# A recurrent attention layer beside a dense layer: weights kept in PSUM as 32-bit words, their copies shared between two engines, queries turned earlier, one load for two row blocks, a wider kept part

## The chip, the cores and the metric

The kernel runs on one core of a Trainium2 chip. The metric is the device time of the whole kernel in microseconds. A core has TensorE (PE; PEld is its loading of weights), VectorE (DVE), ScalarE (ACT), GpSimd (POOL) and SyncE (SP), which here does nothing but start DMA transfers. Transfers are also started from ACT's and POOL's queues.

## What is computed

Two branches over the same normalised input are added to the input. B is a dense layer with GELU; A is attention over segments of 32 tokens, in which each segment also reads 8 memory tokens, and the first 8 rows of its output are the memory of the next segment. So A is a chain of 64 segments, one after the other.

```
xn = layernorm(x)                                   # 2048 x 1024, bf16
out = x + A(xn) + gelu(xn @ w1 + b1) @ w2 + b2      # w1: 1024 x 3584
A:  mem = mem0                                      # 8 x 1024
    for s in range(64):
        h = concat(mem, xn[32 s : 32 s + 32])       # 40 rows
        q, k, v = h @ Wq, h @ Wk, h @ Wv            # 32 heads of 128
        p = softmax(mask(q k^T / sqrt(128)))
        o = (p v) @ Wo                              # back to 1024 columns
        mem = o[0:8];  out of segment s = o[8:40]
```

## The kernel before, in words

**Two stages.** The first stage normalises x, turns it (tokens along the free dimension) and does the dense layer in four groups of 512 tokens. It leaves the turned rows of every segment in a DRAM tensor `hr_d` (columns 0 to 255 of a segment's slot) and the dense result plus input, the residual, in columns 256 to 511 of the slot after it. Then the recurrence runs over 64 segments. To spare PE work, a main tile of 32 rows holds the 8 memory rows and 24 tokens of a segment, and the 8 tokens left over are worked off for four segments together ("left", names with an L, 32 rows per group of four, `i4 = s % 4`): their K, Q, V products are spread over the four segments, and once per group (`left_o`, at `i4 == 1`) the output product is twice as wide.

**Weights.** The four projections are 64 units of 512 KB ([128, 2048] bf16). A segment uses them in the order of `pass_order`: half passes K0, Q0, K1, Q1, V0, V1 of 8 units each, then 16 units of the output product O. SBUF doesn't hold all of them. 46 stay resident; 18 are streamed (`PLACED`, letter S). Six slots form a ring: when PE is done with a streamed unit, `unit_done` calls `start_stream` for the slot that is free now, and SP starts the load of a later unit into it. Two of the 18 never come from DRAM after segment 0: `IN_PSUM` (Q, 4, 0) and `IN_BANKS` (the sixth streamed unit of O, its 15th) are held in four PSUM banks (`kept`) and are copied into their slot by VectorE (L247, two copies of 128x1024 bf16 each); they are started three places later than a load would be, at O's 8th unit for IN_BANKS and K0's first for IN_PSUM. Of a third, `PART` (the fifth streamed of O), the first 512 columns stay in SBUF (`part_home`), and only the rest is loaded (L249). `keep` puts the weights into PSUM in segment 0: PE turns each 128x128 block, ACT and DVE copy the turned blocks to SBUF, PE turns them back into the bank.

**Order.** The program is written out by hand (a manual schedule): each engine runs its instructions in the order of the program, and a half pass takes a table `at`, which says after which unit what else is put in. In segment 0, SP's queue holds, in this order: the last resident units (`xt2`, `xt3`, whose slots are first written out to DRAM as `R_n`), the load of `d_oL` (the second half of IN_BANKS, L605), then the streams. After Q0 the program puts `keep(IN_BANKS)`, the load of `part_home` (L925), and the turning of Q.

**A segment.** A half pass ends with a cast from PSUM by ACT (L758) and, for K and Q, a transposition in 32x32 blocks by VectorE (L772, L939). The queries of the 8 left tokens are put beside the main ones by `q_left` (L794), after Q's half pass. `keep_q` (L801) saves queries that later segments need from being overwritten. `scores` (L808: PE, then Exp on ACT, then two minima on DVE), `sums` (L836: PE sums, Ln and two Exp on ACT, then two products on DVE, L862 and L866, which divide the probabilities) and `values` (L873) run inside later half passes: scores of half 0 after the first unit of Q1, its sums after the last; scores of half 1 after V1's first unit. After V1, the next segment's turned rows are loaded (`load_x_rows`, L259) and, after the first unit of O, the residual (`load_res`, L969): two loads of 64 KB from the same 128 rows of `hr_d`, on ACT's queue up to segment 4, on POOL's from there. O's result is cast (L1002), and `put_mem` (L282 on PE, L286 on DVE) writes the new memory rows into the turned rows, with which the next segment begins. The residual is added (L1017) and POOL stores the rows. For `i4 == 2` they go to a scratch tensor `outM_d` (L1049) and from there to the output (L1052), both on POOL.

**SBUF at fixed places.** Below the pools lie POOL's descriptor space (`SCRATCH`, 512 bytes per partition) and 3584 bytes of small tiles: `half_home` (its columns hold `part_home`, the residual `res_home` and the probabilities `pr_all`), `hr_home` (the turned rows), `pd_main`, `pd_left`, `small_consts`.

Of the kernel before, what the change touches and what calls it, by code (L numbers as in the profile page):

```python
# [11 lines left out]
U32 = mybir.dt.uint32  # L12
# [36 lines left out]
SCRATCH = 512  # L49
SMALL = 3584  # L50
# [4 lines left out]
PART_COLS = 512  # L55
# [31 lines left out]
def kernel(  # L87
# [51 lines left out]
    hr_home = nc.alloc_sbuf_tensor_at("hr_home", [P, 256], BF16, offset=SCRATCH + 2048)  # L139
    pd_main = nc.alloc_sbuf_tensor_at("pd_main", [P, 320], BF16, offset=SCRATCH + 2560)  # L140
    pd_left = nc.alloc_sbuf_tensor_at("pd_left", [P, 128], BF16, offset=SCRATCH + 3200)
    small_consts = nc.alloc_sbuf_tensor_at("small_consts", [P, 16], BF16, offset=SCRATCH + 3456)

    part_home, res_home, pr_all = half_home[:, 0:PART_COLS], half_home[:, 512:768], half_home[:, 768:1024]

    bd, off = small_consts[:, 0:4], small_consts[:, 4:8].bitcast(F32)

# [3 lines left out]
    ctx.enter_context(tc.manual_schedule())  # L151

# [8 lines left out]
    ident = pd_main[:, 0:P]  # L161
# [77 lines left out]

    def start_stream(slot):  # L240
# [4 lines left out]
        if unit in kept_in:  # L245
            for c0, bank in kept_in[unit]:
                nc.vector.tensor_copy(out=t[:, c0:c0 + 1024], in_=bank)  # L247
        elif unit == PART:
            nc.sync.dma_start(out=t[:, PART_COLS:], in_=copies[unit])  # L249
        elif unit in copies:  # L250
            nc.sync.dma_start(out=t[:, :], in_=copies[unit])
        else:
            fetch(t[:, :], unit)
# [4 lines left out]
    def load_x_rows(s, eng=nc.sync):  # L258
        eng.dma_start(out=hr_home[:, :], in_=hr_d[s, :, 0:256])  # L259
        nxt["hT"] = hr_home.rearrange("p (k t) -> p k t", k=KT)  # L260
# [32 lines left out]
    with tc.tile_pool(name="ma", bufs=2) as ma, tc.tile_pool(name="mps", bufs=6, space=PSUM) as mps:  # L293
# [191 lines left out]
        for tg in range(4):  # L485
# [81 lines left out]
            else:  # L567
# [7 lines left out]
                put_mem(o_sb, nxt["hT"], mps.tile([P, 512], F32, name="ps"))  # L575
                pss = [mps.tile([P, 512], F32, name="ps") for _ in range(6)]
# [28 lines left out]
                nc.sync.dma_start(out=d_oL[:, :], in_=Wo_v[:, h + 1, :])  # L605
# [6 lines left out]
    with tc.tile_pool(name="late", bufs=1) as late, \  # L612
# [28 lines left out]
        kept = banks.tile([P, 4, 1024], BF16, name="kept")  # L641

        def copy_bits(out, in_):

            nc.vector.tensor_single_scalar(out=out, in_=in_, scalar=0, op=ALU.bitwise_or)

        def keep(unit, c0, w, bank):

            turned = [late.tile([P, 512], BF16, name=f"VL{n}").rearrange("p (k t) -> p k t", k=4) for n in range(2)]
            for n in range(2):  # L650
                for k in range(4):
                    nc.tensor.transpose(trs[n][:, k, :], w[:, 512 * n + P * k:512 * n + P * (k + 1)], ident)
                (nc.scalar.copy if n else nc.vector.tensor_copy)(out=turned[n], in_=trs[n])
            for n in range(2):
                for k in range(4):
                    c1 = 512 * n + P * k
                    nc.tensor.transpose(kept[:, bank, c1:c1 + P], turned[n][:, k, :], ident)
# [32 lines left out]
        for s in range(NSEG):  # L690
# [145 lines left out]
            def sums(u):  # L836
# [17 lines left out]
                for b in (1, 0):  # L854
# [3 lines left out]
                    )  # L858
                pdA = pd_main.rearrange("p (c b q) -> p c b q", c=4, b=2)
# [38 lines left out]
            def o_product(unit, t, acc):  # L898
# [4 lines left out]
                for k in range(2):  # L903
                    for jq in range(DM // n):
                        r, c0 = n // 8 * jq, DM * k + n * jq
                        w_t = part_home if unit == PART and c0 < PART_COLS else t
                        nc.tensor.matmul(  # L907
                            acc[r:r + n // 8, 0:n],
                            lhsT=lhs[:, 4 * (i % 4) + 2 * u + k, :],
                            rhs=w_t[:, c0:c0 + n],  # L910
                            start=(unit == O_UNITS[0] and k == 0),
                            stop=(unit == O_UNITS[-1] and k == 1),
                            tile_position=(0, r),
                        )


# [4 lines left out]
            psQ, psQL = half_pass("Q", 0, left_q[0], {})  # L921
            if first:
                keep(IN_BANKS, 1024, d_oL, 2)
                keep(IN_BANKS, 0, half_home, 3)
                nc.sync.dma_start(out=part_home, in_=Wo_v[:, 4 * PART[1] + 2 * PART[2], 0:PART_COLS])  # L925
                copy_bits(mixed[:, 468:512].bitcast(U32), mask.bitcast(U32))
                for t in outs:
                    nc.vector.memset(t[:, :, 0:32], 0.0)
                turn_qL(psQL, 0)
            q_left(0)  # L930
            turn_q(psQ)
            if left_q[0] and not first:
                keep_q(0)
# [10 lines left out]
            elif left_k[0]:  # L944
                at[1] = [lambda: turn_kL(psKL, 0)]
            psQ1, psQ1L = half_pass("Q", 1, left_q[1], at)
            if first:
                turn_qL(psQ1L, 1)
            q_left(1)
            turn_q(psQ1)  # L950
            if left_q[1] and not first:
                keep_q(1)
# [7 lines left out]
            at = {0: [lambda: scores(1)], 4: [lambda: sums(1)]}  # L960
# [4 lines left out]

            def load_res():
                st["res"] = res_home
                eng = nc.scalar if s < 5 else nc.gpsimd
                eng.dma_start(out=st["res"][:, :], in_=hr_d[s + 1, :, 256:512])  # L969
# [5 lines left out]
            if not final:  # L975
                load_x_rows(s + 1, nc.scalar if s < 5 else nc.gpsimd)
            if first:
# [9 lines left out]
            at.setdefault(0, []).append(load_res)  # L987
# [105 lines left out]
```

## Time and profile before

The three timed runs gave 1892.51, 1891.93 and 1899.58 us (median 1892.51). The profiled execution took 1888.7 us, with a span of 1887.0 from the first to the last instruction, at a granted TensorE clock of 0.994.

| engine | busy us | share | instructions |
|---|---|---|---|
| PE | 1729.5 | 92% | 32255 |
| PEld | 940.0 | 50% | 32275 |
| DVE | 921.3 | 49% | 2222 |
| ACT | 637.6 | 34% | 1356 |
| POOL | 277.2 | 15% | 538 |

| queue | packets | MB | share of 16 engines |
|---|---|---|---|
| q1 (from SP) | 199292 | 593.57 | 83.0% |
| q0 (from POOL) | 16320 | 17.52 | 2.8% |
| q10 (from ACT) | 4096 | 2.64 | 0.5% |
| instructions (q8, q14) | 317 | 4.66 | 1.0% |

| transfers | count | KB each |
|---|---|---|
| streamed units of K, V, O, Q | 320, 256, 256, 128 | 512 |
| PART | 64 | 384 |
| turned rows, residual (POOL) | 58, 59 | 64 |

Shares are of the span of the slowest core, here the only one. A busy PE isn't PE at its peak, because matmuls overlap and their ends are modelled. A wait for several semaphores is put down to the one that came last. Numbers with an L are lines of the kernel.

### The profile page before, as it was taken

What the parts mean: (1) busy time and instruction counts of PE and PEld (TensorE: products, weight loads), DVE (VectorE), ACT (ScalarE), POOL (GpSimd) and SP (SyncE); (2) the same over time, 40 slices, a digit from 0 to 9 for tenths busy, and PEclk for the clock granted to TensorE, in tenths of its full rate; (3) what the DMA queues carried; (4) which work ended last, traced back from release to release, by engine and by line L of the source; (5) the groups of instructions that cost most, each with busy time, mean ns of one, the idle gap of its engine ahead of it and who ended that gap; (6) DMA issues with size and microseconds to landing.
All of it is one profiled execution on the core that took longest, in us unless ns stands there. A gap on an engine that the chain in (4) does not pass through costs nothing.

```text
span 1887.0 us, 72995 instructions
## 1 busy us (share of the span) xinstructions
PE 1729.5 (92%) x32255; PEld 940.0 (50%) x32275; DVE 921.3 (49%) x2222; ACT 637.6 (34%) x1356; POOL 277.2 (15%) x538
## 2 busy tenths in 40 slices
PE   7999999997998989999999999899999999988987
PEld 3444444444454545455555555455545454555544
DVE  6657474603454444444454445444444454444443
ACT  6334352502333333333333333333333333333332
POOL 0000000000341111111121111212121111111112
PEclk9999999998999999999999999999999999999999
DMA  9821211498999999999999999999999999999998
GB/s 337 269 52 45 55 47 50 172 351 278 401 395 377 372 377 356 378 391 395 391 392 383 387 369 390 370 386 387 385 398 386 392 398 380 387 380 369 376 379 325
DMA packets 220025, 618.39 MB, mean 328 GB/s; under 512 B 47243, under 2 KB 65595, under 8 KB 219708
## 3 DMA queue, kind: packets, MB, share of 16 engines
q1 hardware_dynamic: 199292, 593.57, 83.0%
q0 software_dynamic: 16320, 17.52, 2.8%
q8 instruction: 252, 4.13, 0.9%
q10 hardware_dynamic: 4096, 2.64, 0.5%
q14 instruction: 65, 0.53, 0.1%
HBM read 599.39 MB, written 30.34 MB: 334 GB/s over the span
## 4 chain that ended last, share of the span: by engine, by line
PE 67%; DMA 19%; DVE 7%; ACT 3%; issue 3%; POOL 0%; ACTq 0%; DVEq 0%; POOLq 0%; SPq 0%
PE acc L714 32%; PE ps L503 10%; PE acc L907 10%; DMA u<-Wc_K 9%; PE ps L552 8%; DMA u<-Wc_O 5%; DMA u<-Wc_Q 3%; PE ps L587 2%; ACT mixed L855 2%; PE acc L881 2%; DVE b_oL L772 1%; DMA outL_d<-half_home 1%; DVE pd_main L862 1%; PE mixed L816 1%; DVE u L247 1%
## 5 line engine op out<-in xcount | busy, mean ns | idle before, releaser
L714 PE MATMUL acc<-u,hr_home 128*32 128x512 bf16 x11520 | 781.5, 382 | 32.4 <-DMA u<-Wc_K 13.6
L714 PEld LDWEIGHTS <-hr_home 128*32 128x32 bf16 x12288 | 350.8, 97 | 321.5 <-issue 72.1
L714 PE MATMUL acc<-u,hrL 128*32 128x512 bf16 x2880 | 256.3, 381 | 12.4 <-issue 6.1
L503 PE MATMUL ps<-u 128*128 128x512 bf16 x896 | 194.9, 380 | 2.6 <-ACT u L387 2.6
L907 PE MATMUL acc<-u,d_oL 128*32 128x256 bf16 (+1 forms) x3552 | 177.2, 292 | 12.3 <-DMA u<-Wc_O 7.9
L247 DVE COPY u<-kept 128x1024 bf16<-128x1024 bf16 x254 | 163.3, 685 | 25.7 <-PE acc L907 9.1
L552 PE MATMUL ps<-u 128*128 128x512 bf16 x657 | 146.2, 379 | 0.8
L907 PEld LDWEIGHTS <-b_oL 128*32 128x32 bf16 (+1 forms) x3552 | 109.1, 98 | 75.0 <-issue 40.9
L503 PEld LDWEIGHTS <-u 128*128 128x128 bf16 x896 | 87.9, 98 | 108.4 <-issue 3.1
L907 PEld LDWEIGHTS <-d_oL 128*32 128x32 bf16 (+1 forms) x3552 | 104.4, 99 | 63.8 <-issue 20.7
L862 DVE TENSOR_TENSOR pd_main<-half_home,mixed 128x320 bf16<-128x320 bf16 x128 | 62.5, 488 | 150.1 <-ACT mixed L855 147.6
L907 PE MATMUL acc<-u,b_oL 128*32 128x256 bf16 (+1 forms) x1665 | 108.7, 290 | 19.3 <-DVE u L247 8.8
L714 PEld LDWEIGHTS <-hrL 128*32 128x32 bf16 x3072 | 90.4, 96 | 66.3 <-issue 24.7
L772 DVE STREAM_TRANSPOSE b_oL<-b_oL 128x512 bf16<-128x512 bf16 x128 | 90.6, 708 | 66.8 <-ACT b_oL L758 66.8
L907 PE MATMUL acc<-W_O,b_oL 128*32 128x256 bf16 (+1 forms) x1776 | 108.3, 289 | 4.9 <-issue 4.6
L758 ACT CAST kT<-acc 128x512 bf16<-128x512 f32 x64 | 37.5, 586 | 219.7 <-PE acc L714 219.7
L259 POOL DMA_DIRECT2D hr_home<-hr_d x58 | 32.7, 564 | 528.7 <-PE acc L714 528.7
L552 PEld LDWEIGHTS <-u 128*128 128x128 bf16 x672 | 65.3, 98 | 77.4 <-DVE g_u L519 0.4
L758 ACT CAST b_oL<-acc 128x512 bf16<-128x512 f32 x128 | 75.2, 588 | 80.5 <-PE acc L714 80.5
L833 DVE TENSOR_TENSOR half_home<-half_home,mixed 128x96 bf16<-128x96 bf16 (+1 forms) x256 | 37.6, 188 | 127.4 <-ACT half_home L828 127.3
L1002 ACT CAST d_oL<-acc 128x256 bf16<-128x256 f32 (+1 forms) x63 | 26.9, 427 | 214.2 <-PE acc L907 214.2
L855 ACT ACTIVATE mixed<-mixed,small_consts 128x160 f32<-128x160 f32 x256 | 94.3, 368 | 8.4
(129 smaller groups left out, 2033.3 us busy)
## 6 DMA issues: line engine op xcount, KB each, us to landing
u<-Wc_K SPq DMA_DIRECT2D x320, 512.0 KB
u<-Wc_V SPq DMA_DIRECT2D x256, 512.0 KB
u<-Wc_O SPq DMA_DIRECT2D x256, 512.0 KB
u<-Wc_Q SPq DMA_DIRECT2D x128, 512.0 KB
u<-Wc_O SPq DMA_DIRECT2D x64, 384.0 KB
u<-in_B_w_dram SPq DMA_DIRECT2D x14, 512.0 KB
u<-in_A_Wq_dram SPq DMA_DIRECT2D x14, 512.0 KB
u<-in_A_Wv_dram SPq DMA_DIRECT2D x12, 512.0 KB
```

The source lines that it names most:

```text
L247: nc.vector.tensor_copy(out=t[:, c0:c0 + 1024], in_=bank)
L503: nc.tensor.matmul(ps[:, :].rearrange("p (s t) -> p s t", t=SEG), lhsT=w1_sb[fb // 14 * 8 + kt][:, (fb % 14) * P:(fb % 14 + 1) * P], rhs=x ...
L552: nc.tensor.matmul(ps[:, :], lhsT=gts[fc // 4][:, fc % 4, t * P:(t + 1) * P], rhs=w2_sb[fc // 2][:, fc % 2, cs], start=(fc == 0), stop=(fc ...
L587: nc.tensor.matmul(pss[2 * t + nb][:, :], lhsT=gts[fc // 4][:, fc % 4, t * P:(t + 1) * P], rhs=w2_sb[fc // 2][:, fc % 2, nb * 512:nb * 512 ...
L714: nc.tensor.matmul(o, lhsT=lhs[:, i, :], rhs=m, start=(i == seq[0]), stop=(i == seq[-1]), tile_position=(0, 32 * j),)
L758: cp(out=out, in_=ps.rearrange("p (h e) -> p h e", e=32))
L772: nc.vector.transpose(out=home, in_=home)
L833: nc.vector.tensor_tensor(out=p, in0=p, in1=m[:, None, :].to_broadcast([P, 4, n]), op=ALU.min)
L855: nc.scalar.activation(out=mixed[:, 160 * b:160 * b + 160], in_=mixed[:, 0:160], func=ACT.Exp, scale=-1.0, bias=off[:, b:b + 1],)
L862: nc.vector.tensor_tensor(out=pdA.rearrange("p c b q -> p b c q"), in0=prA[:, None, :, :].to_broadcast([P, 2, 4, 40]), in1=dd, op=ALU.mult,)
L881: nc.tensor.matmul(oV[r][:, c, :, :], lhsT=V[q, c * P:(c + 1) * P], rhs=pdA[q, c, :, :], start=(c == 0), stop=False, skip_group_check=True ...
L907: nc.tensor.matmul(acc[r:r + n // 8, 0:n], lhsT=lhs[:, 4 * (i % 4) + 2 * u + k, :], rhs=w_t[:, c0:c0 + n], start=(unit == O_UNITS[0] and k ...
```

## The change

1. `PART_COLS` goes from 512 to 768: of PART's 2048 columns 768 stay in SBUF and 1280 are loaded per segment. The product of L907 takes the tile in which the border falls in two parts of 256 columns.
2. `keep` copies the weights to PSUM bit for bit, as 512 words of 32 bits, in one VectorE instruction per bank. IN_BANKS is kept before the first half pass of segment 0 instead of after Q0; the load of `d_oL` goes to where `put_mem` is done in the first stage, ahead of the last resident units in SP's queue.
3. Of the two copies of a kept unit into its slot, VectorE does the first as words and ScalarE the second as bf16.
4. `q_left` and `keep_q` go into the half pass of Q (after its third and fourth unit), ahead of the turning of Q; the two divisions of half 0 (`normalize`) go after the turning of Q1.
5. `load_x_rows` loads 512 columns, rows and residual together (segment 0's own rows excepted), after V1; `load_res` goes. `res_home` lies in `hr_home` now.
6. The transfer from `outM_d` to the output goes from POOL's to SP's queue and to the next segment, after the third unit of O.
7. `SCRATCH` goes from 512 to 384 bytes; `pd_left` and `small_consts` move into a pool.

```diff
-SCRATCH = 512
-SMALL = 3584
+SCRATCH = 384
+SMALL = 3712
...
-PART_COLS = 512
+PART_COLS = 768
...
             for c0, bank in kept_in[unit]:
-                nc.vector.tensor_copy(out=t[:, c0:c0 + 1024], in_=bank)
+                if c0:
+                    nc.scalar.copy(out=t[:, c0:c0 + 1024], in_=bank.bitcast(BF16))
+                else:
+                    copy_bits(t[:, c0:c0 + 1024].bitcast(U32), bank.bitcast(U32))
...
     def load_x_rows(s, eng=nc.sync):
-        eng.dma_start(out=hr_home[:, :], in_=hr_d[s, :, 0:256])
+        n = 512 if s else 256
+        eng.dma_start(out=hr_home[:, 0:n], in_=hr_d[s, :, 0:n])
...
                 put_mem(o_sb, nxt["hT"], mps.tile([P, 512], F32, name="ps"))
+                nc.sync.dma_start(out=d_oL[:, :], in_=Wo_v[:, h + 1, :])
...
         def keep(unit, c0, w, bank):
 
-            turned = [late.tile([P, 512], BF16, name=f"VL{n}").rearrange("p (k t) -> p k t", k=4) for n in range(2)]
-            for n in range(2):
-                for k in range(4):
-                    nc.tensor.transpose(trs[n][:, k, :], w[:, 512 * n + P * k:512 * n + P * (k + 1)], ident)
-                (nc.scalar.copy if n else nc.vector.tensor_copy)(out=turned[n], in_=trs[n])
-            for n in range(2):
-                for k in range(4):
-                    c1 = 512 * n + P * k
-                    nc.tensor.transpose(kept[:, bank, c1:c1 + P], turned[n][:, k, :], ident)
+            copy_bits(kept[:, bank, :].bitcast(U32), w.bitcast(U32))
...
+            if first:
+                keep(IN_BANKS, 1024, d_oL, 2)
+                keep(IN_BANKS, 0, half_home[:, :], 3)
+                nc.sync.dma_start(out=part_home, in_=Wo_v[:, 4 * PART[1] + 2 * PART[2], 0:PART_COLS])
...
             psK, psKL = half_pass("K", 0, left_k[0], {})
...
-            psQ, psQL = half_pass("Q", 0, left_q[0], {})
+            at = {} if first else {2: [lambda: q_left(0)]}
+            if left_q[0] and not first:
+                at[3] = [lambda: keep_q(0)]
+            psQ, psQL = half_pass("Q", 0, left_q[0], at)
...
-            q_left(1)
+                q_left(1)
             turn_q(psQ1)
+            normalize(0)
...
-            at = {0: [lambda: scores(1)], 4: [lambda: sums(1)]}
+            at = {0: [lambda: scores(1)], 4: [lambda: sums(1), lambda: normalize(1)]}
...
-            at.setdefault(0, []).append(load_res)
+            if i4 == 3:
+                at.setdefault(2, []).append(rows_of_main)
...
-                small.append(lambda o=o, r=r: nc.gpsimd.dma_start(out=o, in_=r))
+                rows_of_main = lambda o=o, r=r: nc.sync.dma_start(out=o, in_=r)
```

## The prediction

> **What bounds the kernel now.** I read the profile in this order: the DMA rows of the 40 slices, the stage windows, the records of single DMA packets, the chain of waits at the start of the recurrence, the waits. Page, part 2:
>
> ```profile
> DMA  9821211498999999999999999999999999999998
> GB/s 337 269 52 45 55 47 50 172 351 278 401 395 377 372 377 356 378 391 395 391 392 383 387 369 390 370 386 387 385 398 386 392 398 380 387 380 369 376 379 325
> ```
>
> From slice 11 on (some 470 us to the end) the 16 DMA engines are never below 90%. The dense half ahead of it is TensorE's, with DMA at a tenth or two; the change hardly touches it. Windows (length; busy us of PE, PEld, DVE, ACT, POOL; clock; DMA share; GB/s):
>
> ```profile
> 445.00:450.00 5.00, 3.06 (x64) 1.62 (x56) 3.16 (x8) 1.69 (x5) 0.00 (x0) 1.00 0.71 234
> 450.00:455.00 5.00, 4.60 (x56) 2.02 (x60) 1.87 (x4) 0.00 (x0) 0.00 (x0) 0.66 0.23 61
> 455.00:460.00 5.00, 4.74 (x124) 2.38 (x116) 1.49 (x4) 1.89 (x5) 0.00 (x0) 1.00 0.56 188
> 460.00:465.00 5.00, 4.82 (x144) 3.71 (x140) 2.97 (x6) 1.46 (x4) 0.71 (x1) 1.00 0.84 242
> ...
> 900.00:1000.00 100.00, 93.36 (x2176) 53.21 (x2172) 49.40 (x119) 33.96 (x79) 16.80 (x32) 1.00 1.01 393
> ```
>
> Steady segments have a DMA share of 1.01, so DMA sets their period. The casts of L1002, one at each segment's end, start from 465.6 to 1858.9 us: 62 periods of 22.47 us. VectorE is half busy and ScalarE a third. PE shows 93%, but its matmuls overlap (382 ns each, four started every 0.21 us), so this isn't PE at its limit: it waits often, and briefly. Counting in the packet records how many of 16 packets are in service at each ns between 500 and 1800 us leaves 2.0% of engine time free, 26 us: all that anything but DMA could still win there. The exception is segment 0 (418.9 to 465.6 us), where the windows above show idle DMA. Its chain:
>
> ```profile
> 419.54 8.30 DMA R_n<-u
> ...
> 428.34 4.43 DMA d_oL<-in_A_Wo_dram
> ...
> 432.82 0.41 PE mixed L652 x4
> ...
> 438.51 0.56 DVE qL L758
> ...
> 439.11 4.31 PE acc L714 x30
> ```
>
> SyncE's queue stands until 427.9 us for the write of R_n, then loads d_oL; PE waits for d_oL only to transpose it into PSUM, and the second half pass of K starts 20 us after the first.
>
> **What the Trainium skill says.** "ScalarE: Activation LUTs", What ACT_TABLE_LOAD costs: an ACTIVATE with immediate scale and bias is 186 ns + 0.833 ns per element. The trace agrees: casts from PSUM take 372 ns at 256 columns, 586 at 512. "VectorE: DVE Perf Modes", Why PSUM operands drop a tier: 32-bit data in PSUM goes at single rate. The trace's word copies into PSUM (L645) agree: 200 ns at 64 words, 267 at 128, so 1.05 ns a word. "DMA: Bandwidth & Descriptors", Issuing engines are not separate DMA queues: SP, ACT and POOL share the same 16 DMA engines; the one share near 1.00 agrees. The same page, Why a DMA increments its semaphore by 16 and not by 1: a DMA runs on the largest k up to 16 that divides the slowest dimension of both sides; from SP always on the lowest-numbered k, from POOL on k that rotate. The trace fits k = 4 for outM to out, whose slowest dimension is 4: it went as 12 packets of 4096 bytes, not a multiple of 16. Which engines they were, it doesn't show.
>
> **The change part by part.**
>
> *768 columns kept.* The load of PART shrinks from 384 to 320 KB: 128 packets of 2560 instead of 3072 bytes, once per segment. Mean packet times between 500 and 1800 us: 2048 bytes 86.4 ns, 3072 128.1, 4096 168.3. Halfway, 2560 takes 107.3. Saving: 128 x 20.8 ns / 16 engines = 0.166 us; with the medians (84, 121) 0.148; by bytes, 65.5 KB at 385 GB/s, 0.170. I take 0.16 us, times 64 loads = **-10.2 us**. It lies on the path, DMA being the bound. The wider product of L907 is cut in two for one tile in 16 segments: the same columns stream, nothing.
>
> *Weights kept as words.* Gone from segment 0: 64 transposes and 8 copies, with PE's waits between them (425.2 to 429.4, and from 432.8 until PE gets its bank at 439.1 after the qL cast queued behind). In their place four VectorE copies of 512 words, 267 + 384 x 1.05 = 0.67 us each: two ahead of segment 0, where VectorE is idle for 4.2 us before L772 at 423.1, two beside the Q pass. PE then runs into the SyncE queue: the first load after 427.9 us lands some 6 us later (estimate: 1.2 MB with what is ahead of it, 3.1 us at 400 GB/s, plus 2.9, which d_oL took beyond the 0.78 MB then queued: 432.8 - 427.9 - 2.0); PE would be there at 431, so segment 0 becomes DMA-bound from 428 on. What is saved is the DMA idle time after that: (0.29 + 0.77 + 0.44 + 0.16) x 5 = 8.3 us in the windows above. I take 8.0, and 0.5 for the 256 KB of d_oL, which move to before 420 us where DMA stood at 0.6, less 64 KB more for part_home: **-8.5 us**. Bounds: -4 (a second wait, such as the hrL load of 5.6 us) to -10.
>
> *Copies back shared.* Per segment four copies of 685 ns on VectorE (L247, two pairs) become two of 0.67 there and two on ScalarE. No row shows a ScalarE copy of 1024 columns: 586 + 512 x 0.833 = 1.01 us. A pair is ready after 1.01 instead of 1.37 us. Behind it on ScalarE stand the kT cast and L1002, before which ScalarE is idle 219.7/64 and 214.2/63 = 3.4 us: hidden. PE's wait for these copies is 8.8 us in all, part of the 2% slack: **0**, bounds -3 to +1.
>
> *Queries first.* q_left (0.15 to 0.20 us) and keep_q (0.20 to 0.27) move into the pass, beside its matmuls. The divisions (0.49 + 0.28) of half 0 now queue on VectorE behind the transposition of L772, which itself waits for ScalarE's 0.59 us cast. Before: Ln and two Exp, 1.1 us, divisions and q_left 0.8, transposition 0.63. Now 1.1, cast 0.59, transposition 0.63: PE's scores come 0.2 us earlier, values(0) 0.1 later, and where a qL cast follows (one segment in four) the bank comes free 0.4 later. All inside PE's slack: **0**, bounds -6 (part of the 16.3 us of the wait below) to +6 (16 x 0.4).
>
> *One load for rows and residual.* On ACT in the first five segments, on POOL afterwards. The bytes stay and a 64 KB load is already 16 packets of 4096, so DMA gains nothing; POOL saves an issue of 0.55 us, hidden. But put_mem (L286) now waits for 128 KB, one more packet per engine and one of the stream between: 0.33 us later. Landing is 5.2 us now. Behind the waiting L286 stand L1017 and the next copies on VectorE, and PE's next pass waits for it. Segment by segment, PE's last put_mem matmul ends between 0.6 us before and 3.4 after the landing; 0.3 us more adds 2.3 us over all segments. Half is hidden by DMA: **+1**, bounds 0 to +6 (0.9 us later, as if both came one after the other: 12.6, halved).
>
> *Rows of main on SP.* The store outM to out (one segment in four) leaves POOL, whose 5.3 us wait for outM goes; on SP it is issued 16 us later and waits for nothing; the issue, about 0.6 us like SP's other DRAM copies, falls into SyncE's waits for slots. It is 96 packets of 512 bytes (27 ns from the ACT queue). Spread evenly: 0.0. On the same four engines: 24 x 27 = 0.65 us against 12 x 162/16 = 0.12, +0.53 x 16 = +8.4. I take **0**, bounds 0 to +8.4, since the trace names no engine.
>
> *Moved addresses, POOL's smaller descriptor space*: no instruction changes; POOL is busy 15%. 0.
>
> Sum: -10.2 - 8.5 + 1 = **-17.7 us**, 1869.3 for the profiled span of 1887.0. The three timed runs have a median of 1892.5, so I predict 1874.8.
>
> **Rivals.** The other waits in question (who, for whom: us, times, longest):
>
> ```profile
> DVE hr_home L286 <- DMA hr_home<-hr_d: 10.7, 5, 2.6
> ...
> PE acc L907 <- DVE u L247: 8.8, 14, 0.7
> ```
> ```profile
> PE mixed L816 <- DVE b_oL L772: 16.3, 26, 0.7
> ```
>
> 1. *Four engines become the bound.* The SP store always lands on the same four engines: 1874.8 + 8.4 = 1883.2. For it: DMA has no slack. Against: if other engines lag already, it is hidden.
> 2. *Steady segments follow PE's chain of latencies, not bytes*: only segment 0 gains: 1892.5 - 8.5 + 1 = 1885.0. For it: periods differ by type (some 24 us where the wide output product runs, 21 to 23 elsewhere). Against: the share of 1.01.
> 3. *Slower: the merged load.* If 128 KB land d later, put_mem and so the whole chain moves. From the segments' own slacks the waits sum to 28.0 us at d = 1.4 and 50.0 at d = 2.0. From d = 1.4 on (18.7 + 9.5 = 28.2) the kernel is slower by over 0.5%; at 2.0 it ends at 1892.5 - 18.7 + 50 = 1924. For it: 5 waits exist already. Against: POOL's loads land in 5.0 to 5.8 us from 12 to 64 KB alike.
> 4. *It doesn't do what it says*: PE still starts segment 0's second half late (another wait for the same queue): 1892.5 - 10.2 + 1 = 1883.3.
>
> **How the numbers follow.** Forecast 0.70, rival 1 0.10, rival 2 0.08, rival 3 0.06, rival 4 0.06. Low end: the sum with its gains at their bounds, -10.9 - 10 - 3 - 6 = -29.9, hardly all at once; I take -28: 1864. High end: the forecast with segment 0 at -4 plus the four engines, -10.2 - 4 + 1 + 8.4 = -4.8: 1887. That takes in rivals 1, 2 and 4. A measurement tells about 0.5% (9.5 us) from no change: faster means below 1883.0. Forecast 0.70 and half of rivals 1 and 4, which end near that line, give faster 0.78; their other half and rival 2 same 0.16; rival 3 slower 0.06.
>
> **What would show it.** Right: 3072-byte packets gone, 2560 at about 107 ns; the segment period at 22.3 us; share still 1.00; segment 0 ends near 457 us without idle DMA. Wrong: periods of 22.47 with DMA share below 0.99 (rival 2); SyncE waiting for DMA more often with 2% more free engine time (rival 1); longer waits of L286 (rival 3).

## The result and the profile after

| | us, median | range | runs |
|---|---|---|---|
| before | 1892.22 | 1891.34 to 1899.58 | 4 |
| after | 1911.47 | 1907.54 to 1911.70 | 4 |

The ratio is 1.0088, with a 95% interval of 1.006 to 1.0117: the change made the kernel slower by some 17 us, where a gain of 17.7 was forecast. The profiled span went from 1887.0 to 1910.0 us, at a granted clock of 0.99 in both.

One window of segment 0 in the kernel after (columns as in the prediction), and then the whole steady stretch, before and after:

```profile
450.00:455.00 5.00, 4.96 (x119) 3.01 (x120) 1.88 (x6) 1.97 (x5) 0.71 (x1) 1.00 1.03 411
```
```profile
500.00:1800.00 1300.00, 1185.89 (x27464) 677.79 (x27463) 617.32 (x1461) 424.34 (x983) 236.25 (x440) 1.00 1.00 384
```
```profile
500.00:1800.00 1300.00, 1159.27 (x27000) 656.19 (x26994) 536.45 (x1323) 530.50 (x1081) 190.91 (x362) 1.00 0.99 374
```

Segment 0 did what was forecast: from 450 to 455 us the engines' share is 1.03 where it was 0.23 before, and the windows beside it have 1.02 and 1.03. But in the steady stretch 374 GB/s move instead of 384 (part of this is the 64 KB per segment that are no longer loaded), at a share that fell by one hundredth only, and PE is busy 1159 us of 1300 instead of 1186. PE and the transfers both do less per microsecond, so the time is to be looked for in waits. (The prediction's window from 900 to 1000 us, with PE at 93.36, was the busiest of those around it before.)

The casts that end the segments (L1002 before, L1006 after) say in which segments. Times in us; the last four columns are means over the segments from 6 on, by `i4`:

| | segment 0 ends | period of segments 1, 2, 3, 4, 5 | mean from 6 on | i4 = 0 | 1 | 2 | 3 |
|---|---|---|---|---|---|---|---|
| before | 465.6 | 23.47, 21.61, 22.57, 22.25, 23.98 | 22.445 | 21.80 | 23.84 | 21.35 | 22.87 |
| after | 458.7 | 22.68, 28.89, 24.47, 22.86, 23.69 | 22.808 | 22.01 | 23.38 | 21.52 | 24.41 |

Three things stand out. Segment 0 ends 6.9 us earlier (what that hides is said under e12). Segment 2 is 7.3 us longer. And the segments with `i4` = 3 are 1.54 us longer, 16 times. Within these, one stretch takes nearly all of it: from the cast of K1 to the cast of Q1, 3.17 us before and 4.69 after.

That stretch, once, on VectorE, with the two PE groups that matter (timeline: start, duration, line, operation, tiles, and idle time ahead of it with what ended it). Before:

```profile
1060.32 0.70 DVE L939 STREAM_TRANSPOSE d_oL<-d_oL 128x512 bf16<-128x512 bf16 x1
1060.90 0.26 PE L841 MATMUL mixed<-half_home,small_consts 128*32 128x160 bf16 x4
1061.64 0.71 DVE L772 STREAM_TRANSPOSE kL<-kL 128x512 bf16<-128x512 bf16 x1
1062.40 0.49 DVE L862 TENSOR_TENSOR pd_main<-half_home,mixed 128x320 bf16<-128x320 bf16 x1
1062.81 0.28 DVE L866 TENSOR_TENSOR pd_left<-half_home,mixed 128x128 bf16<-128x128 bf16 x1
1063.01 0.22 DVE L794 COPY b_oL<-mixed 128x128 bf16<-128x128 bf16 x1
1063.14 0.70 DVE L772 STREAM_TRANSPOSE b_oL<-b_oL 128x512 bf16<-128x512 bf16 x1
1063.89 0.20 PE L816 MATMUL mixed<-b_oL,d_oL 128*32 128x40 bf16 x4 [0.55 <-DVE b_oL L772]
```

and the same segment after, where both PE groups wait for another instruction:

```profile
1069.86 0.70 DVE L940 STREAM_TRANSPOSE d_oL<-d_oL 128x512 bf16<-128x512 bf16 x1
1071.17 0.71 DVE L767 STREAM_TRANSPOSE kL<-kL 128x512 bf16<-128x512 bf16 x1
1071.81 0.18 DVE L789 COPY b_oL<-mixed 128x128 bf16<-128x128 bf16 x1
1072.05 0.25 PE L836 MATMUL mixed<-half_home,small_consts 128*32 128x160 bf16 x4 [1.42 <-DVE b_oL L789]
1074.07 0.71 DVE L767 STREAM_TRANSPOSE b_oL<-b_oL 128x512 bf16<-128x512 bf16 x1 [2.08 <-ACT b_oL L753]
1074.71 0.45 DVE L859 TENSOR_TENSOR pd_main<-half_home,mixed 128x320 bf16<-128x320 bf16 x1
1075.08 0.28 DVE L863 TENSOR_TENSOR pd_left<-half_home,mixed 128x128 bf16<-128x128 bf16 x1
1075.41 0.20 PE L811 MATMUL mixed<-b_oL,d_oL 128*32 128x40 bf16 x4 [0.92 <-DVE pd_left L863]
```

Before, PE's sums (L841) ran at 1060.90, and Ln and Exp on ScalarE lay beside VectorE's work on the left keys. After, `q_left` (L789) has moved up in the program, but on VectorE it stands behind the turn of the left keys (L767 into `kL`) and the cast before that (0.65 us). It reads queries out of the PSUM tile `mixed` (columns from 340 on), and the sums (L836) write to `mixed` (columns 0 to 159). The columns don't meet, but in the program's order the sums come after `q_left`, and PE waits for it. The wait shows 14 times from 500 to 1800 us, as often as segments with `i4` = 3 fall there, the only ones in which this `q_left` reads `mixed`. So ScalarE's chain starts only when VectorE is through with the left keys. The second new wait stands at the end: the divisions (L859, L863) read columns 0 to 319 of `mixed`, and the scores of half 1 (L811) write to 0 to 223, so the scores come after the divisions although they don't use them. From the turn of the natural keys (L939 at 1060.32 before, L940 at 1069.86 after) to the scores (L816 at 1063.89, L811 at 1075.41) it took 3.57 us before and 5.55 after. Over the steady stretch, 500 to 1800 us, after (who, for whom: us, times, longest):

```profile
PE mixed L811 <- DVE pd_left L863: 40.0, 42, 1.1
PE mixed L836 <- DVE b_oL L789: 19.2, 14, 1.4
PE mixed L836 <- DVE mixed L241: 9.4, 13, 1.2
```

The third is `keep_q` (it goes through the helper of L241) in the segments with `i4` = 2. Before, the same stretch had 16.3 us of PE waiting for the turn of Q and 9.1 for `keep_q`, and none of the three above.

Segment 2 has another cause. The chain of work there, after:

```profile
498.21 1.82 issue
500.04 5.49 DMA hr_d<-R_n
...
505.55 6.43 DMA hr_home<-hr_d
...
512.07 0.23 DVE hr_home L293
```

POOL still issues the first stage's writes of the residual to `hr_d`, with gaps in which it waits for no semaphore that the trace shows ("issue"; e8 says what ends them). The merged load of rows and residual must wait for such a write, and the new memory rows (L293), and PE behind them, for the load.

My theory at this point: part 4 lost some 20 us by the order on VectorE, part 7 some 7 us by slowing POOL's issues, segment 0 gained as forecast, and the 64 KB gave nothing. The rivals: four DMA engines that the store on SP overloads (rival 1 of the prediction), and the bytes.

### The profile page after: what moved, and what is told of

Same layout as the page of the kernel before. It is cut to its first block, busy times and chain, and to the rows that moved or that the text cites. A ratio compares the mean times of both kernels' runs of the same rounds, so it can differ in the third digit from the quotient of the medians.

```text
span 1910.0 us, 73084 instructions
## 1 busy us (share of the span) xinstructions
PE 1722.2 (90%) x32228; PEld 926.0 (48%) x32228; DVE 843.7 (44%) x2095; ACT 760.5 (40%) x1479; POOL 233.4 (12%) x464
## 4 chain that ended last, share of the span: by engine, by line
PE 37%; DMA 21%; DVE 6%; ACT 5%; issue 4%; POOL 1%; ACTq 0%; DVEq 0%; POOLq 0%
PE acc L709 24%; DMA u<-Wc_K 11%; PE acc L906 9%; DMA outL_d<-half_home 4%; DMA u<-Wc_O 2%; DMA u<-Wc_Q 2%; PE acc L878 2%; ACT mixed L850 2%; DVE d_oL L940 1%; ACT b_oL L753 1%; DVE pd_main L859 1%; PE mixed L811 1%; DVE kL L753 1%; ACT half_home L823 1%; ACT mixed L847 1%
## 5 line engine op out<-in xcount | busy, mean ns | idle before, releaser
L709 PEld LDWEIGHTS <-hr_home 128*32 128x32 bf16 x12288 | 346.8, 96 | 333.1 <-issue 68.6
L251 ACT COPY u<-kept 128x1024 bf16<-128x1024 bf16 x127 | 128.5, 1012 | 177.9 <-DVE u L241 112.8
L906 PE MATMUL acc<-u,d_oL 128*32 128x256 bf16 (+1 forms) x3552 | 172.7, 290 | 8.0 <-issue 5.0
L767 DVE STREAM_TRANSPOSE b_oL<-b_oL 128x512 bf16<-128x512 bf16 x128 | 91.1, 712 | 168.1 <-ACT b_oL L753 168.0
L906 PEld LDWEIGHTS <-b_oL 128*32 128x32 bf16 x3569 | 110.6, 98 | 72.8 <-issue 39.3
L241 DVE TENSOR_SCALAR u<-kept 128x512 uint32<-128x512 uint32 x127 | 87.7, 691 | 86.0 <-ACT u L251 63.0
L847 ACT ACTIVATE mixed<-mixed 128x160 f32<-128x160 f32 x128 | 36.9, 288 | 170.7 <-PE mixed L842 170.7
L518 ACT ACTIVATE g_xb<-ps,b1col 128x512 bf16<-128x512 f32 x112 | 76.8, 686 | 61.2 <-PE ps L510 60.1
L859 DVE TENSOR_TENSOR pd_main<-half_home,mixed 128x320 bf16<-128x320 bf16 x128 | 59.9, 468 | 93.0 <-ACT mixed L850 93.0
L767 DVE STREAM_TRANSPOSE kT<-kT 128x512 bf16<-128x512 bf16 x64 | 45.5, 711 | 124.3 <-ACT kT L753 124.3
```

The costliest lines, as they stand in the source:

```text
L251: nc.scalar.copy(out=t[:, c0:c0 + 1024], in_=bank.bitcast(BF16))
L518: nc.scalar.activation(out=xb[:, :], in_=ps[:, :], func=ACT.Identity, bias=b1col[:, fb:fb + 1], scale=1.0)
L709: nc.tensor.matmul(o, lhsT=lhs[:, i, :], rhs=m, start=(i == seq[0]), stop=(i == seq[-1]), tile_position=(0, 32 * j),)
L767: nc.vector.transpose(out=home, in_=home)
L847: nc.scalar.activation(out=mixed[:, 0:160], in_=mixed[:, 0:160], func=ACT.Ln)
L859: nc.vector.tensor_tensor(out=pdA.rearrange("p c b q -> p b c q"), in0=prA[:, None, :, :].to_broadcast([P, 2, 4, 40]), in1=dd, op=ALU.mult,)
```

## The experiments

The ratios are to the kernel before on the same chip. Undoing a part starts from the kernel after unless something else is said.

**e1_queries_back.** Part 4 undone.

```diff
-            at = {} if first else {2: [lambda: q_left(0)]}
...
+            q_left(0)
...
-                7: [lambda: sums(0)],
+                7: [lambda: sums(0), lambda: normalize(0)],
...
-            normalize(0)
```

> The changed kernel with its part 4 alone undone: q_left and keep_q after the half passes of Q, both divisions inside sums, as before the change. Theory Q (the query order is the main loss: PE's sums of half 0 wait for q_left behind the left keys' turning on VectorE, and the scores of half 1 wait for the divisions): the K1-to-Q1 stretch of the segments with i4 = 3 falls from 4.69 back to about 3.2 us and that of i4 = 2 from 4.34 to 3.8; 1911.5 - 16 x (1.5 + 0.5) and some of the 0.2 us elsewhere: 1870 to 1885 us. Theory M (the merged load is the main loss): about 1905 to 1911 us. Theory B (DMA is the bound in steady segments, as forecast): within 5 us of 1911.

Measured: 1890.06 us (20 runs), ratio 0.9977 (0.9958 to 0.9996). The mean period is 22.375 us, at `i4` = 3 22.79, and K1 to Q1 there 3.14 us. Segment 2 stays at 28.64. Against the 1.0088 of the kernel after, part 4 is 0.011 of the time, some 21 us.

**e2_two_loads.** Part 5 undone.

```diff
-        n = 512 if s else 256
+        n = 256
...
+            at.setdefault(0, []).append(load_res)
```

> The changed kernel with its part 5 alone undone: rows (64 KB) after V1, residual (64 KB) after O's first unit. Theory M: the lost 7.3 us of segment 2 and 1.9 of segment 3 come back, and the 0.3 to 0.4 us from the end of O to the end of K0 in 48 segments as well: 1911.5 - 9 - 15 = about 1888 us. Theory Q: only the early segments come back: 1900 to 1905 us.

Measured: 1943.75 us (4 runs), ratio 1.0261 (1.0203 to 1.0319), mean period 23.372: 32 us slower than after, where both theories had expected a gain. Waits of this run, 500 to 1880 us:

```profile
DVE half_home L1025 <- DMA half_home<-hrL_d: 37.3, 14, 4.4
PEld L709 <- DVE hr_home L1025: 26.3, 14, 3.6
```

The left residual comes late (once per group of four, at `i4` = 1), VectorE waits for it in the addition (L1025), and PE's next pass behind that. Its load is the third of three that POOL issues in a row: rows, residual, left residual. Here is the third in this run, and in the kernel before:

```profile
1042.79 0.53 POOL L1005 DMA_DIRECT2D half_home<-hrL_d  x1 [4.84 <-issue]
```
```profile
1024.92 0.54 POOL L997 DMA_DIRECT2D half_home<-hrL_d  x1 [0.32 <-issue]
```

In the 15 groups from 560 us on, the last of the run left out, POOL stands 3.7 to 5.5 us ahead of this third load in e2, and in each of them it goes on 0.33 us after the first of the three has landed. (The profile puts 12 of these stands down to a copy on another engine that ended at about that time; the landing fits all 15.) Before, with 512 bytes, it went on after 0.1 to 0.3 us, without waiting for a landing. So with 384 bytes POOL has two such loads under way at a time here, with 512 three. Part 7 is still in this kernel; e10 takes it out.

**e3_rows_on_12_engines.** The store on SP with tokens outermost, so that by the rule that the prediction names it would spread over 12 engines. The trace names none.

```diff
-                o = out_flat[rows, :].rearrange("t (j c) -> j t c", j=4)
-                r = outM_d[g, :, :].rearrange("(j t) c -> j t c", j=4)[:, 0:NX, :]
+                o = out_flat[rows, :].rearrange("t (j c) -> t j c", j=4)
+                r = outM_d[g, :, :].rearrange("(j t) c -> t j c", j=4)[0:NX, :, :]
```

> The changed kernel with the transfer from outM to the output still on SP, but with its 24 rows outermost[...] (same 96 packets of 512 bytes). If the four engines were a bound (rival 1 of the prediction): 5 to 8 us faster, 1903 to 1906 us. If not: within 2 us of 1911.5.

Measured: 1913.39 us (9 runs), ratio 1.0103 (1.007 to 1.0136), mean period 22.795 against 22.808. The 5 to 8 us that rival 1 asked for don't come; no cost of the store is seen where it is.

**e4_keep_512.** `PART_COLS` 512, all else as after.

> The changed kernel with 512 instead of 768 columns of PART kept (PART loads of 384 KB again). If bytes set the period of the steady segments: 0.16 us x 64 = 10 us slower, 1921 us. If PE's chain of waits sets it in the changed kernel: under 3 us slower, 1911 to 1914 us.

Measured: 1914.74 us (12 runs), ratio 1.0095 (1.0067 to 1.0123), mean period 22.798. In the kernel after, 64 KB more per segment cost 3 us by the medians, which can't be told from zero.

**e5_divisions_back** and **e6_q_left_back.** Part 4 halved: in e5 `normalize(0)` stands behind the sums again, in e6 `q_left` and `keep_q` stand after the pass of Q again.

> The changed kernel with only the divisions of half 0 put back into sums (ahead of the turning of Q1); q_left and keep_q stay inside the half passes. If the sums' wait for q_left and keep_q is the loss: the K1-to-Q1 stretch stays at 4.7 us for i4 = 3 and 4.3 for i4 = 2, PE's 45 us of waits of the scores for pd_left go, and the span stays above 1900 us. If the late divisions are the loss: the span falls to about 1885 us.

> The changed kernel with q_left and keep_q put back after the half passes, the divisions of half 0 still behind the turning of Q1. If the sums' wait for q_left is the loss: K1-to-Q1 back to 3.2 us for i4 = 3, and the span near 1885 to 1890 us, while PE's scores go on waiting some 45 us for pd_left, hidden by DMA. If the late divisions are the loss: above 1900 us.

Measured: e5 1897.99 us (10 runs), 1.0026 (0.9999 to 1.0053); e6 1895.79 us (18 runs), 0.9995 (0.9974 to 1.0017). In e5 the wait for the divisions is gone and that for `q_left` stays; K1 to Q1 at `i4` = 3 is still 4.69 us, and 4.08 at `i4` = 2 instead of 4.34. In e6 it is the other way round, and K1 to Q1 falls to 3.30. PE's waits from 500 to 1800 us: for `q_left` (L836) 21.3 us, 15 times, in e5; for the divisions (L811) 28.0 us, 29 times, in e6.

Both expectations asked which half is the loss; it is both. Against e1 (0.9977) the early `q_left` costs 0.005 and the late divisions 0.002, which is within the intervals; both together 0.011. That both cost more than their sum would fit the order (late sums make late divisions, for which the scores then wait), but the intervals are too wide to show it.

**e9_queries_back_keep_512** and **e8_space_512.** e9 is e1 with `PART_COLS` 512. e8 is e9 with part 7's smaller space undone (three small tiles change their places for it).

```diff
-SCRATCH = 384
-SMALL = 3712
+SCRATCH = 512
+SMALL = 3584
```

> The changed kernel with part 4 undone and 512 columns of PART kept: against e1 it measures the bytes once PE's chain is as before. If DMA sets the period then: 0.16 us x 64 = 10 us slower than e1 (span about 1890). If the chain of waits sets it there as well: within 3 us of e1's 1880.8.

> The changed kernel with part 4 undone, POOL's descriptor space back at 512 bytes, and 512 columns of PART kept (to make room; pd_left lies in half_home, pd_main and the left rows swap places). If POOL's small descriptor space makes the residual's writes late, and the merged load waits for them: segment 2 falls from 28.6 to about 22 us, segment 3 by 0.5, and the span is 7 us below e9. If the merged load waits for those writes whatever the space: segment 2 stays at 28 us.

Measured: e9 1892.22 us (12 runs), 0.999 (0.9961 to 1.0018); e8 1886.62 us (20 runs), 0.9953 (0.9935 to 0.9972). e9 against e1 is the bytes once more: 2 us by the medians for 64 KB, not 10, and within the intervals. From e9 to e8 segment 2 falls from 30.32 to 21.75 us, and segment 3 from 22.98 to 22.05. POOL's waits put down to "issue" between 478 and 512 us, e9 and then e8:

```profile
POOL hr_d L458 <- issue: 10.1, 3, 4.8
POOL half_home L995 <- issue: 3.7, 1, 3.7
```
```profile
POOL hr_d L458 <- issue: 4.7, 4, 1.7
```

With 512 bytes the load of the left residual (L995) no longer stands behind the writes. In all it is 5.6 us by the medians, with intervals that just overlap, and some 9 us by segments 2 and 3.

What settles it are all the profiles together. In the nine kernels with 384 bytes segment 2 takes 27.3 to 30.3 us, and between 430 and 560 us POOL stands 44 to 52 us in "issue" waits of over 1 us. In the ten profiles with 512 bytes it is 20.8 to 22.2 us, and POOL stands 10 to 22 us. Both groups have kernels with one load and with two, and the small tiles lie in two ways among those with 512, so neither the merged load nor the places make the difference. And the waits tell what they are for: in e9 each of the 15 ends 0.30 to 0.35 us after the third, fourth or fifth transfer before it on POOL has landed, in e8 each of the 7 after the fifth, sixth or seventh. With less space, fewer of POOL's transfers are under way at a time. (Single waits can be long with 512 bytes too, up to 6.7 us in e10: what differs is the sum.)

**e7_small_space_split_early.** e1 with a load of its own for the residual in the first five segments only, on ACT's queue, so that the load of the rows need not wait for the residual's writes.

> Edit: changed kernel with part 4 undone (as in e1), 768 columns and the smaller space for POOL's descriptors kept; in the first five segments the residual has a load of its own on ACT's queue after O's first unit, so that the turned rows of the next segment no longer wait for the residual's writes. Theory (POOL's queue of writes, held up by the smaller space, makes the merged load wait in segment 2 only): segment 2 falls from 28.6 to 21.5-22.5 us, everything else as in e1, so some 6.5 us below e1's 1890 on the same chip: ratio to before 0.994. Rival (the writes delay segment 2 by another way, such as the DMA engines being full of them): segment 2 stays above 27 us and the ratio at 0.998. Rival 2 (the residual's own load comes late now and its addition holds up VectorE and PE): segment 3 grows to above 26 us.

Measured: 1890.04 us (22 runs), 0.9978 (0.996 to 0.9996); segment 2 is 29.79. My theory of the merged load as the one victim falls. The late issues (POOL stands 11.9 us at four of them) hit the next in the queue, here the left residual; the waits for it between 478 and 516 us:

```profile
DVE half_home L1021 <- DMA half_home<-hrL_d: 8.0, 1, 8.0
PEld L709 <- DVE hr_home L1021: 7.2, 1, 7.2
```

**e10_space_512_two_loads**, run twice. e8 with two loads and the store of the main rows on POOL again: parts 2 and 3 stay, with some moved tiles.

> Edit: e8 with two loads again (rows after V1, residual after O's first unit) and the store of main rows back on POOL: so what stays of the change is the weights as words, the earlier load of d_oL and the shared copies back. Theory (the two loads cost 32 us in e2 only because the smaller space left POOL's queue no room): same as e8 within 3 us, mean of the segments from 5 on 22.35-22.55. Rival (merged load is a gain of its own, also with the larger space): e8 better by 10 us or more, mean above 22.6. Rival 2 (the merged load costs its one more packet per engine, the +1 to +6 of the prediction): e10 faster than e8 by 1 to 6 us.

> The kernel of e10 once more, beside e13 and e14 on the same chip. Expected: ratio to before 0.994 as then, 0.991 to 0.997, mean of the segments from 5 on 22.4-22.6.

Measured: 1884.38 us (12 runs), 0.9936 (0.9909 to 0.9964), and 1884.50 us (22 runs), 0.9962 (0.9939 to 0.9985). With 512 bytes two loads are as good as one (e8). Between e2 and e10 lie part 4 and the wider kept part as well, but the stand ahead of the third load is gone here (0.32 us by the median in place of 4.4), so e2's 32 us were the price of two loads together with the smaller space.

**e11_space_512_copies_back.** e8 with both copies on VectorE as bf16.

```diff
-                if c0:
-                    nc.scalar.copy(out=t[:, c0:c0 + 1024], in_=bank.bitcast(BF16))
-                else:
-                    copy_bits(t[:, c0:c0 + 1024].bitcast(U32), bank.bitcast(U32))
+                nc.vector.tensor_copy(out=t[:, c0:c0 + 1024], in_=bank.bitcast(BF16))
```

> Edit: e8 with both copies of a kept unit on VectorE as bf16 (part 3 undone), nothing else. Theory (the two copies write one tile and run one after the other either way, 1.70 us shared against 1.37 us on VectorE alone, and the slots have slack): same as e8 within 3 us. Rival (sharing gains: VectorE is free 1.4 us per segment for turns and additions that PE waits for): e11 slower than e8 by 5 us or more, mean of the segments from 5 on above 22.58. Rival 2 (sharing costs: pair ready 0.3 us later and ScalarE's casts queue behind 1.0 us copies): e11 faster than e8 by 4 us or more, mean below 22.40.

Measured: 1882.64 us (13 runs), 0.9935 (0.9912 to 0.9958), beside 0.9953 for e8. Sharing the copies gives nothing that can be told from zero. In the kernel after, ScalarE's copy waits for VectorE's (112.8 us over the run) or the other way round (63.0), since both write one tile.

**e12_only_words_before_segment_0.** The kernel before with part 2 alone.

> Edit: kernel before with part 2 alone (weights put into PSUM by one VectorE copy of words per bank, ahead of segment 0, with the load of d_oL moved up). Theory (segment 0's gain is the one part of the prediction that holds): segment 0 ends 7 to 11 us earlier, steady segments at 22.4-22.5 as before; ratio to before 0.995, 0.994 to 0.997. Rival (POOL's or SP's queue gives it back in the next segments, since they start earlier into the same queue of writes): segments 1 to 5 longer by 4 us or more in sum, ratio 0.998 or above.

Measured: 1888.57 us (21 runs), 0.9959 (0.9937 to 0.9981): 7.8 us off 1895. Periods as before, 22.502 on the mean. Yet in the profile segment 0 ends at 462.6 us, 3.0 us earlier and not 7 to 11. The reason lies ahead of it. In this execution, as in that of the kernel after, the granted clock was 0.50 from 369 to 375 us, where it was 1.00 before (14 matmuls in these 6 us instead of 29), and the first half pass started at 423.3 and 423.1 us instead of 419.0. The change doesn't do that: e10 and e10b are the same kernel, and start at 418.8 without and at 422.8 with such a stretch. From its own start segment 0 is 7.3 us shorter in e12 than before, 11.1 in the kernel after, and between these and 11.7 in all profiles with part 2. The chain of segment 0 here:

```profile
427.41 3.45 PE acc L706 x60
...
433.06 6.80 DMA u<-Wc_Q
...
439.91 4.89 PE acc L706 x56
```

PE goes straight from the first half pass (from 423.26 us) into the second, and then waits for the second load behind SyncE's long stand, 6.8 us: what the prediction said of it.

**e13_no_part_kept.** e10 with `PART_COLS` 0, so 128 KB more per segment than e10.

> Edit: e10 with PART_COLS 0, so that PART's load is 512 instead of 384 KB, 128 KB more per segment (two packets of 4096 instead of 3072 bytes' worth per engine and row: 128 x (168.3 - 128.1) ns / 16 = 0.32 us by the packet times of before). Theory A (bytes set the steady period, as predicted): 0.32 us more per segment, 20 us in all, ratio to e10b 1.010 to 1.011. Theory B (PE's chain of latencies sets it, the DMA engines' share near 1.0 being occupancy): no change, within 4 us of e10b. In between (bytes set some of the segments' stretches): 5 to 15 us.

Measured: 1887.45 us (22 runs), 0.9967 (0.9946 to 0.9988), against 1884.50 and 0.9962 for e10b beside it: 1 to 3 us more, uncertain by some 6, where bytes as the bound would give 20. Windows from 500 to 1800 us, e10b and then e13:

```profile
500.00:1800.00 1300.00, 1186.40 (x27500) 679.81 (x27492) 550.89 (x1348) 538.78 (x1099) 233.69 (x435) 1.00 1.00 384
```
```profile
500.00:1800.00 1300.00, 1175.38 (x27240) 680.32 (x27240) 546.34 (x1336) 534.45 (x1090) 229.27 (x427) 0.99 1.01 387
```

A share of 1.00 was not the most that the engines move. The profiles alone would mislead here: mean periods are 22.634 for e13, 22.410 for e10b, and 22.598 for e10, which is the same kernel as e10b. So one profile's mean is good to about 0.2 us, by these two.

**e14_queries_first_alone.** e10 with part 4 alone.

> Edit: e10 with part 4 alone (q_left and keep_q inside the pass of Q, the divisions of half 0 after the turning of Q1). Theory (part 4 is the loss, by itself: with i4 = 3 the scores of half 1 wait for a late division and the sums of half 0 for a late q_left): the stretch K1 to Q1 at i4 = 3 grows from 3.1-3.3 to 4.5-4.8 us, i4 = 2 by 0.3-0.6, mean of the segments from 5 on up by 0.3-0.45 us, 18 to 27 us over e10b, ratio 1.010 to 1.014 to it. Rival (it needed the smaller space or the wider kept part): within 6 us of e10b. Rival 2 (bytes refill the gap): K1 to Q1 grows, but other stretches shrink, under 10 us.

Measured: 1904.37 us (12 runs), 1.0065 (1.0039 to 1.0091): 19.9 us over e10b. Stretches between casts at `i4` = 3: K1 to Q1 4.69 us against 3.14; the period 24.37 against 22.72; at `i4` = 0, 1 and 2 it is 22.20, 23.35 and 21.22 against 22.26, 23.27 and 21.47. PE's waits, e14 and then e10b (`pd_left` lies in `half_home` here):

```profile
PE mixed L811 <- DVE half_home L863: 39.7, 42, 1.1
PE mixed L836 <- DVE b_oL L789: 22.2, 16, 1.4
PE mixed L836 <- DVE mixed L241: 5.2, 9, 1.2
```
```profile
PE mixed L811 <- DVE b_oL L767: 16.0, 26, 0.7
PE mixed L811 <- DVE mixed L241: 9.2, 14, 0.7
```

The same three waits as in the kernel after, the first two of about the same size and the third of half, without the smaller space and without the wider part. They sum to 67.1 us in place of 25.2; of the 41.9 us more, 19.9 reach the end.

**e15_q_left_ahead_of_left_keys** and **e16_same_copies_back.** Queries early in another place: e10 with `q_left` after the first unit of the pass of Q, ahead of the left keys; divisions and `keep_q` where they were before. e16 has both copies on VectorE too.

```diff
-                0: [lambda: scores(0), lambda: nc.vector.transpose(out=nat_home, in_=nat_home)],
+                0: [
+                    lambda: scores(0), lambda: first or q_left(1),
+                    lambda: nc.vector.transpose(out=nat_home, in_=nat_home),
+                ],
```

> Edit: e10 with q_left of each half moved into the pass of Q, but after its first unit (half 1: behind the scores of half 0 and ahead of the turning of the left keys), keep_q and the divisions where they were before the change. Theory (the place in VectorE's order is what costs): no new wait of PE's sums for q_left; q_left's 0.14 to 0.22 us leave the path from the cast of Q to the scores, twice per segment; K1 to Q1 at i4 = 3 stays at 3.1-3.2 us; same as e10 (0.9936, 0.9962 of before) or up to 12 us faster, ratio 0.988 to 0.996. Rival (any early q_left costs, since it makes the sums' writer of the shared PSUM tile wait for a reader on VectorE): K1 to Q1 at i4 = 3 above 3.6 us, ratio above 0.999.

> Edit: e15 with both copies of a kept unit on VectorE as bf16. Theory (copies have slack either way, as e11 against e8): within 5 us of e15. Rival (VectorE's order is what counts now, and two copies of 0.69 us more per pair hold up q_left): slower than e15 by over 5 us.

Measured: e15 1887.88 us (21 runs), 0.9951 (0.9931 to 0.9972); e16 1884.38 us (10 runs), 0.9943 (0.9921 to 0.9965). PE no longer waits for `q_left`; K1 to Q1 at `i4` = 3 is 3.17 us in e15. The early queries neither cost nor gain here. What costs is where they stand in VectorE's order, and the late divisions.

**The best version.** e8, e10, e11, e15 and e16 lie at 0.9935 to 0.9962 with intervals that overlap: 7 to 12 us faster than before, and some 1.4% faster than the kernel after. e12, the kernel before with part 2 alone, can't be told from them.

## Why the prediction was wrong

- **Queries first, "all inside PE's slack: 0".** This step failed, by 20 us (e1, e14). It counted the durations ahead of the scores about right: Ln and Exp, cast, transposition. But it assumed that they would start as early as before, and that the scores would follow the transposition. Both have a wait on `mixed` that the step didn't look for: the sums, which write to it, wait for the early `q_left`, which on VectorE stands behind 1.3 us of left keys; and the scores of half 1, which write to it, wait for the late divisions. The bound of +6 had priced only a bank that comes free later.
- **Moved addresses, POOL's smaller descriptor space: 0.** Failed, by some 5.6 us (e9 to e8). "POOL is busy 15%" is no measure of room for its transfers: the loss lies where many are issued in a row, behind the first stage, and not in the mean. The profile before had a sign of it: from 430 to 560 us POOL stood 16.7 us in "issue" waits of over 1 us, with 512 bytes.
- **768 columns, -10.2.** Failed: e4 and e9 show 2 to 3 us that can't be told from zero, and e13 1 to 3 us for twice the bytes, so at most some 4 of the 10.2 (half of e13's upper end). The step took the share of 1.01 for a bound. The packets show it too: those of 2560 bytes took 120 ns on the mean (102 by the median), not 107, and SP's of 4096 169.4 ns instead of 168.3. Rival 2, that steady segments follow PE's chain and not the bytes, was nearer to this, with a chance of 0.08. It isn't the whole either: of the waits that e14 adds to that chain half reach the end. Its time, 1885.0, was missed because the chain itself was made longer.
- **Weights as words, -8.5.** Right in mechanism and size: -7.8 in e12 (some 4 to 12 by its interval). In the profile after, segment 0 ends 6.9 us earlier although SyncE was held until 432.5 us instead of 427.9. That is the later start of the execution, told under e12: in e10 SyncE goes on at 428.0, in e10b, the same kernel, at 432.1.
- **Copies shared, 0.** Right within what can be measured (e11, e16), but not as argued: the pair isn't ready after 1.01 us, since the two copies run one after the other, 0.69 and 1.01 us. The duration of ScalarE's copy was foreseen to the nanosecond, because it was carried on from the measured 586 ns. The formula named beside it gives 399 and 612 ns for the casts of 256 and 512 columns, where the trace has 372 and 586: its slope agrees, its constant is 27 ns too high here.
- **The merged load, +1**, and **rows of main on SP, 0.** e8 and e10 differ by less than their intervals, and e3 shows no cost of four engines. The merged load lands 5.42 us after its issue by the median, where the rows alone took 5.19: 0.23 us for 0.33 priced. Rival 3 had its victim, the wait of L293 (L286 before), but not as priced: it isn't that loads take 1.4 us longer, but that the source of one is written late, in segment 2.

The sum with the measured terms: -7.8 + 20 + 5.6 = +17.8 us; measured 0.0088 x 1892 = +16.7. Each term is uncertain by several us, so that they meet this closely is in part luck.

The 26 us of free engine time that were "all that anything but DMA could still win" misled twice. They bound gains and not losses, and the bound itself rested on the share.

## What to carry to other kernels

Before an instruction is moved up in a program, list what stands ahead of it on its own engine at the new place, and who writes next to any tile that it reads: here a 0.18 us copy, moved ahead, held up TensorE by 1.4 us, because a later group wrote to another part of the same PSUM tile. At a place ahead of the left keys it cost nothing (e15). A transfer share near 1.00 says that the engines are occupied, not that they set the period; add bytes, measure, and only then price a saving. A queue's room is judged in the stage that issues most, not by the engine's mean.

## What the runs showed of the hardware

- With 384 instead of 512 bytes per partition for its transfers, POOL has fewer of them under way: of three loads of 64 KB in a row the third is issued 0.33 us after the first has landed, 3.7 to 5.5 us late (e2); with 512 bytes it follows after 0.3 us (before, e10). With one more load per segment in that queue the whole kernel loses 32 us (e2), with the larger space none (e10).
- 128 KB more per segment move within 3 us of the same time in the medians of 22 runs each, uncertain by some 6, with the engines' share at 1.00 and 1.01 (e10b, e13).
- VectorE copies a bank as 512 words of 32 bits in 691 ns; as 1024 columns of bf16 it took 685 before: words gain nothing there. ScalarE takes 1012 ns for 1024 columns.
